# A fused attention, gated convolution, Fourier mixing and FFN kernel on one core: the second FFN group's norm starts at the thirteenth block, and two groups' deviations are inverted as 128x4

## The chip, the cores and the metric

The kernel runs on one core of one Trainium2 chip. The metric is the device time of one execution in microseconds. Three runs of the kernel before gave 1488.09, 1489.01 and 1493.40 us; the median is 1489.01 us.

Engines in the profile: PE is TensorE (matmuls; PEld its weight loads), DVE is VectorE, ACT is ScalarE, POOL is GpSimd, SP is SyncE, which here only issues transfers (DMAs).

## What is computed

Eight batches of 576 tokens with 512 features go through block-causal attention, a gated causal convolution, and then the part that the change touches:

```python
def _moe2_ref(x, w_ch1, w_ch2):
    X = np.fft.fft(np.fft.fft(x, axis=1), axis=2)
    u = x + np.real(X).astype(np.float32)
    mu = np.mean(u, axis=-1, keepdims=True)
    var = np.mean((u - mu) ** 2, axis=-1, keepdims=True)
    un = (u - mu) / np.sqrt(var + 1e-06)
    ch = np.maximum(un @ w_ch1, 0.0) @ w_ch2        # 512 -> 2048 -> 512
    return (u + ch).astype(np.float32)
```

## The kernel before

`phase1` computes attention, convolution and Fourier mixing batch by batch and stores u transposed (features by tokens) in DRAM as `u_d`. `phase2`, the FFN, takes the 4608 tokens in nine groups (g) of 512. A group holds u as `U` (four tiles of 128 features by 512 tokens). Since the ReLU is positively homogeneous, the division by the deviation is left to the end: the matmuls work on u minus its mean, and the result is multiplied by the row `RS[g]`, one over the deviation, spread over 128 partitions.

**A block.** The 2048 hidden features are 16 blocks (f, 0 to 15; the first is block 0). Block f has 12 matmuls into `psh` (lines 1172 to 1174), ACT's ReLU `hh` (1177), DVE's remainder `hl` (1178), and 12 matmuls into four accumulators `o` (1190 to 1192), which PE does one block later, after the `psh` of block f+1. Every f32 product is done as three products of a rounded high part and a low part (H and L in the names). The third of each trio on `o` (line 1192) reads `hl`.

**Weights.** Group 0 also prepares the weights. For each block, `load_w` loads two 128x1024 pieces `rw` of raw 64-bit numbers (line 1081, three buffers), which are decoded to f32: one ACT instruction (80), four DVE instructions (72, 74, 76, 84), then ACT rounds (1085) and DVE takes the remainder (1086). That is ten DVE instructions a block beside `hl`. Groups 1 to 8 find the weights in place.

**The norm.** `norm(g)` is a generator; the block loop takes one step of it a block (`next(nxt, None)`). Its steps: the sum of four tiles (lines 1129 to 1131); the mean by a matmul with a matrix of 1/512 (`average`: L1106 in group 0, and otherwise L1111 and L1112 to split, L1114 and L1115 to multiply); four steps, each x = u - mean (1138), its rounded part `UTH` (1139, ACT), the remainder `UTL` (1140) and the square added to `q` (1142, 1144); the mean of the squares, again by `average`, into `pv`; the root (1149, ACT) and `reciprocal` of 128x512 numbers that are alike in all partitions (1150, DVE). For g below 2, `pool` is DVE, so the whole norm but its ACT steps is DVE work; from group 2 on POOL takes part of it. Group g+1's norm begins in block 5 of group g, or in block 8 where g is 0. The first six steps of group 0's norm are placed in front by a priority.

**What sets the order.** The code is recorded, and a scheduler then fixes the order of every engine's instructions by its own estimates; each engine runs its list in that order and waits at the first instruction that isn't ready. So group 0 runs beside the end of `phase1`. DVE's list mixes decoding, `hl`, the norm of group 1 and the last additions of the Fourier part (842, some of them on POOL). SP's list mixes the loads of `rw` with the last stores of `u_d` (847) and the loads of `U` (1098).

At a group's end each `o` is multiplied by `RS[g]` (1199, DVE), u is added (1201, POOL) and the result stored (1202).

Of the kernel before, what the change touches and what calls it, by code (L numbers as in the profile page):

```python
# [8 lines left out]
F32 = mybir.dt.float32  # L9
F32R = mybir.dt.float32r  # L10
AF = mybir.ActivationFunctionType
# [6 lines left out]
def kernel(  # L18
# [13 lines left out]
    nc = tc.nc  # L32
    B, NP, P, S = q.shape
# [57 lines left out]
    dram = ctx.enter_context(tc.tile_pool(name="dram", bufs=1, space=bass.MemoryType.DRAM))  # L91
    u_d = [dram.tile([D, S], F32, name=f"u_d{b}") for b in range(B)]

    f_d = [dram.tile([10, P], F32, name=f"f_d{i}") for i in range(2)]

    cst = ctx.enter_context(tc.tile_pool(name="cst", bufs=1))
# [945 lines left out]
    def phase2():  # L1042
        with ExitStack() as c2:
# [7 lines left out]
            T = 512  # L1051
            N0X = 6
            OFF = 150
            NG = NTOK // T
            s3 = sb("s3", 3)
            rp = sb("rp", 3)
# [61 lines left out]
            def norm(g):  # L1118

                if g >= NG:  # L1120
                    return
                UTH[g] = UHS[g % 2]
                UTL[g] = ULS[g % 2]
                u = U[g]

                pool = nc.gpsimd if g > 1 else nc.vector
                s1 = s2.tile([P, T], F32, tag="x", name="s1")
                s = s2.tile([P, T], F32, tag="x", name="s")
                nc.vector.tensor_tensor(out=s1, in0=u[:, 2, :], in1=u[:, 3, :], op=ALU.add)
                pool.tensor_tensor(out=s, in0=u[:, 0, :], in1=u[:, 1, :], op=ALU.add)  # L1130
                nc.vector.tensor_tensor(out=s, in0=s, in1=s1, op=ALU.add)
                yield
                pm = ps_t.tile([P, T], F32, tag="t", name="pm")
                yield from average(g, pm, s)
                q = s5.tile([P, T], F32, tag="s", name="q")
                for t in range(4):
                    x = s2.tile([P, T], F32, tag="x", name="x")
                    nc.vector.tensor_tensor(out=x, in0=u[:, t, :], in1=pm, op=ALU.subtract)
                    nc.scalar.copy(out=UTH[g][:, t, :], in_=x)
                    (pool if t % 2 else nc.vector).tensor_tensor(  # L1140
                        out=UTL[g][:, t, :], in0=x, in1=UTH[g][:, t, :].bitcast(F32), op=ALU.subtract)
                    nc.scalar.activation(out=x if t else q, in_=x, func=AF.Square)
                    if t:
                        pool.tensor_tensor(out=q, in0=q, in1=x, op=ALU.add)
                    yield
                pv = ps_t.tile([P, T], F32, tag="t", name="pv")
                yield from average(g, pv, q)
                RS[g] = r = s5.tile([P, T], F32, tag="r", name="r")
                nc.scalar.activation(out=r, in_=pv, func=AF.Sqrt, bias=eps)
                nc.vector.reciprocal(out=r, in_=r)  # L1150
                yield
# [6 lines left out]
            for g in range(NG):  # L1158
# [3 lines left out]
                for f in range(NF + 1):  # L1162
                    if g == 0 and f + 2 < NF:
                        load_w(f + 2)
                    if f == 2:
                        load_u(g + 1)
                    if f == (5 if g else 8):
                        nxt = norm(g + 1)
                    if f < NF:
                        ps = ps_h.tile([P, T], F32, tag="h", name="psh")  # L1170
                        for c in range(4):
                            nc.tensor.matmul(ps, W1H[f][:, c * P:c * P + P], UTH[g][:, c, :], start=(c == 0), stop=False)  # L1172
                            nc.tensor.matmul(ps, W1H[f][:, c * P:c * P + P], UTL[g][:, c, :], start=False, stop=False)  # L1173
                            nc.tensor.matmul(ps, W1L[f][:, c * P:c * P + P], UTH[g][:, c, :], start=False, stop=(c == 3))  # L1174
                        h = HH[f % 2]
                        l = HL[f % 2]
                        nc.scalar.activation(out=h, in_=ps, func=AF.Relu)  # L1177
                        nc.vector.scalar_tensor_tensor(out=l, in0=ps, scalar=0.0, in1=h.bitcast(F32),  # L1178
                                                       op0=ALU.max, op1=ALU.subtract)
                        hs[f] = (h, l)  # L1180
                    next(nxt, None)
                    if f == 0 or g == NG - 1 and f == NF - 1:
                        continue

                    es = list(hs) if f == NF else [f - 1]
                    for t in range(4):
                        c = slice(t * P, (t + 1) * P)
                        for e in es:
                            h, l = hs[e]
                            nc.tensor.matmul(po[t], W2H[e][:, c], h, start=(e == 0), stop=False)  # L1190
                            nc.tensor.matmul(po[t], W2L[e][:, c], h, start=False, stop=False)  # L1191
                            nc.tensor.matmul(po[t], W2H[e][:, c], l, start=False, stop=(e == NF - 1))  # L1192
                    for e in es:
                        del hs[e]
# [105 lines left out]
```

## Time and profile before

| | |
|---|---|
| median of three runs | 1489.01 us (1488.09 to 1493.40) |
| the profiled execution's own time | 1489.86 us |
| its span, first to last instruction | 1488.1 us |
| PE busy | 1425.6 us, 96% of the span |
| DVE busy | 832.4 us, 56% |
| ACT busy | 645.7 us, 43% |
| POOL busy | 309.4 us, 21% |

The shares are averages over stages with different limits. In the 40 slices of the page, DVE's busy tenths are 9 in slices 18 to 21 (about 670 to 818 us: the end of `phase1` and group 0), and 1 or 2 in the slices after, while PE's are 9 nearly throughout. A stretch has to be read by itself: which engine waits there, and for whom.

A row by stretch gives the stretch, its length, the busy time of PE, PEld, DVE, ACT and POOL with their numbers of instructions, the granted TensorE clock (1.00 is 2.4 GHz, 0.50 is 1.2 GHz), the DMA engines' busy share and GB/s. In a timeline row the columns are the start, the duration, the engine, the line and operation with output<-inputs, the shape, how many instructions of one kind were merged (x1, x2), and in brackets the engine's idle time just before and who ended it. A recorded DVE instruction of 128x512 lasts 0.68 us, but the next one starts about 0.60 us after it started; the step from start to start is the price.

### The profile page before, as it was taken

The page shows a single profiled execution, that of the slowest core. Times are in us where ns is not written, and L with a number is a line of the kernel's source. Part 1 is how long each engine was busy: PE and PEld are TensorE (multiplying, and loading weights), DVE is VectorE, ACT ScalarE, POOL GpSimd, SP SyncE. Part 2 cuts the span into 40 slices and gives each one's busy share as a digit, 9 for nine tenths or more (in the row PEclk, how much of TensorE's full clock was granted, in tenths as well). Part 3 has the DMA queues.
Part 4 walks back from the last instruction along what each step waited for, and adds up shares of the span by engine and source line. Part 5 has one row for each costly group of instructions (what it writes and reads, how often), then busy time and mean ns, then how long its engine had stood idle before and what let it go on. Part 6 is the DMA issues. An engine that isn't in the chain of part 4 may idle for free.

```text
span 1488.1 us, 22958 instructions
## 1 busy us (share of the span) xinstructions
PE 1425.6 (96%) x8543; PEld 1207.0 (81%) x8543; DVE 832.4 (56%) x1688; ACT 645.7 (43%) x1655; POOL 309.4 (21%) x254
## 2 busy tenths in 40 slices
PE   5798999999999999999989999999999999999998
PEld 3567888989998999887768888888888888888887
DVE  6777797979797979899992222222222222222212
ACT  5677777777877777643441212121121212112110
POOL 3423232323232323221001111110111111011100
PEclk9899999999999999999999999999999999999999
DMA  7557665656565656244521010100101000010000
GB/s 216 156 154 198 161 177 147 170 149 170 152 171 147 170 152 167 80 132 134 164 74 43 1 57 0 57 0 1 57 0 57 0 30 27 1 57 0 29 0 29
DMA packets 121612, 137.23 MB, mean 92 GB/s; under 512 B 23567, under 2 KB 91421, under 8 KB 121501
## 3 DMA queue, kind: packets, MB, share of 16 engines
q1 hardware_dynamic: 120960, 135.63, 32.2%
q8 instruction: 67, 1.10, 0.3%
q14 instruction: 45, 0.36, 0.1%
q10 hardware_dynamic: 540, 0.14, 0.0%
HBM read 70.57 MB, written 19.01 MB: 60 GB/s over the span
## 4 chain that ended last, share of the span: by engine, by line
PE 67%; DVE 14%; issue 5%; DMA 4%; ACT 4%; POOL 3%; SPq 1%; DVEq 0%; ACTq 0%; POOLq 0%
PE o L1192 7%; PE psh L1172 7%; PE psh L1174 7%; PE psh L1173 7%; PE o L1190 7%; PE o L1191 7%; PE av L609 4%; PE pt L581 3%; DVE gate L636 2%; PE sc L421 2%; PE sc L422 2%; PE psx L182 1%; PE psx L183 1%; PE psx L184 1%; DVE mx L453 1%
## 5 line engine op out<-in xcount | busy, mean ns | idle before, releaser
L1178 DVE SCALAR_TENSOR_TENSOR hl<-psh,hh 128x512 fp32r<-128x512 f32 x144 | 99.2, 689 | 398.9 <-ACT hh L1177 398.9
L1177 ACT ACTIVATE hh<-psh 128x512 fp32r<-128x512 f32 x144 | 85.9, 597 | 494.0 <-PE psh L1174 493.8
L1192 PE MATMUL o<-hl,W2H 128*128 128x512 f32 x504 | 194.3, 392 | 8.2 <-DVE hl L1178 8.1
L1174 PE MATMUL psh<-UTH,W1L 128*128 128x512 f32 x504 | 196.9, 391 | 0.0
L1173 PE MATMUL psh<-UTL,W1H 128*128 128x512 f32 x504 | 196.7, 390 | 0.0
L1172 PE MATMUL psh<-UTH,W1H 128*128 128x512 f32 x504 | 196.7, 390 | 0.0
L1190 PE MATMUL o<-hh,W2H 128*128 128x512 f32 x504 | 196.1, 389 | 0.0
L1191 PE MATMUL o<-hh,W2L 128*128 128x512 f32 x504 | 196.0, 389 | 0.0
L467 ACT ACTIVATE PB<-sc,mx 128x128 f32<-128x128 f32 (+4 forms) x320 | 166.7, 526 | 48.3 <-DVE mx L453 28.6
L581 PE MATMUL pt<-ident,PB 128*128 128x128 f32 x800 | 139.4, 280 | 12.1 <-ACT PTb L587 5.8
L636 DVE SCALAR_TENSOR_TENSOR gate<-XF,cw,gate 128x575 f32<-128x575 f32 (+3 forms) x128 | 121.7, 951 | 5.1 <-ACT gate L63 4.4
L581 PEld LDWEIGHTS pt<-ident,PB 128*128 128x128 f32 x800 | 100.1, 143 | 28.4 <-ACT PTb L587 12.5
L1192 PEld LDWEIGHTS o<-hl,W2H 128*128 128x128 f32 x504 | 94.1, 188 | 32.0 <-DVE hl L1178 12.8
L1201 POOL TENSOR_TENSOR U<-o,U 128x512 f32<-128x512 f32 x32 | 40.4, 1294 | 354.4 <-DVE o L1199 354.4
L1172 PEld LDWEIGHTS psh<-UTH,W1H 128*128 128x128 f32 x504 | 95.0, 189 | 20.0
L1173 PEld LDWEIGHTS psh<-UTL,W1H 128*128 128x128 f32 x504 | 95.0, 189 | 19.9
L1174 PEld LDWEIGHTS psh<-UTH,W1L 128*128 128x128 f32 x504 | 94.9, 188 | 19.7
L1190 PEld LDWEIGHTS o<-hh,W2H 128*128 128x128 f32 x504 | 94.6, 188 | 19.9 <-ACT hh L1177 0.4
L1191 PEld LDWEIGHTS o<-hh,W2L 128*128 128x128 f32 x504 | 94.6, 188 | 19.8
L453 DVE TENSOR_REDUCE mx<-sc 128x1 f32<-128x384 f32 (+2 forms) x192 | 104.2, 560 | 3.8 <-PE sc L184 1.9
L421 PE MATMUL sc<-K,QQ 128*128 128x256 f32 (+2 forms) x256 | 87.8, 353 | 15.4 <-DMA QQ<-QHL 11.7
L632 POOL TENSOR_TENSOR XL<-XF,XH 128x576 fp32r<-128x576 f32 x32 | 46.4, 1451 | 259.5 <-ACT XH L57 259.3
(233 smaller groups left out, 3151.0 us busy)
## 6 DMA issues: line engine op xcount, KB each, us to landing
K<-KP SPq DMA_DIRECT2D x128, 144.0 KB, 2.5
QQ<-QHL SPq DMA_DIRECT2D x128, 128.0 KB, 2.4
rw<-in_w_ch SPq DMA_DIRECT2D x28, 512.0 KB, 4.3
VV<-in_v SPq DMA_DIRECT2D x32, 320.0 KB, 4.0
qraw<-in_q SPq DMA_DIRECT2D x32, 288.0 KB, 3.1
kraw<-in_k SPq DMA_DIRECT2D x32, 288.0 KB, 3.4
out<-U SPq DMA_DIRECT2D x36, 256.0 KB, 2.0
QQ<-QHL SPq DMA_DIRECT2D x128, 64.0 KB, 2.8
```

The source lines that it names most:

```text
L421: nc.tensor.matmul(t[:, o:o + w], q[:, 0, m], KK[p][h][:, 0:w], start=True, stop=False)
L453: nc.vector.reduce_max(out=mx[:, j:j + 1], in_=t, axis=AX.X, negate=one)
L467: nc.scalar.activation(out=PB[i][:, k0:k0 + w], in_=t, func=AF.Exp, bias=nm, accum_out=su[:, at + j:at + j + 1])
L581: nc.tensor.transpose(ps[:, j, :], PB[i][:, (j0 + j) * P:(j0 + j + 1) * P], ident)
L636: nc.vector.scalar_tensor_tensor(out=gate[c][:, s:S], in0=XF[:, 0:S - s], scalar=cw[:, c, 4 - s:5 - s], in1=gate[c][:, s:S], op0=ALU.mult, ...
L1172: nc.tensor.matmul(ps, W1H[f][:, c * P:c * P + P], UTH[g][:, c, :], start=(c == 0), stop=False)
L1173: nc.tensor.matmul(ps, W1H[f][:, c * P:c * P + P], UTL[g][:, c, :], start=False, stop=False)
L1174: nc.tensor.matmul(ps, W1L[f][:, c * P:c * P + P], UTH[g][:, c, :], start=False, stop=(c == 3))
L1178: nc.vector.scalar_tensor_tensor(out=l, in0=ps, scalar=0.0, in1=h.bitcast(F32), op0=ALU.max, op1=ALU.subtract)
L1190: nc.tensor.matmul(po[t], W2H[e][:, c], h, start=(e == 0), stop=False)
L1191: nc.tensor.matmul(po[t], W2L[e][:, c], h, start=False, stop=False)
L1192: nc.tensor.matmul(po[t], W2H[e][:, c], l, start=False, stop=(e == NF - 1))
```

## The change

Four things change, all in `phase2`.

1. Group 1's norm starts in block 12 instead of 8 (`NL = 12`), and from there group 0's loop takes two steps of it a block.
2. Group 1's `U` is asked for in block 9 of group 0 instead of block 2.
3. For groups 0 and 1 the mean of the squares is taken by four matmuls with `q` as the weights and one column of 1/512, so that `pv` holds 128x4 numbers, token 128j + p in partition p. The root and `reciprocal` are done on 128x4.
4. These 512 numbers are written to a DRAM tile `r_d` and read back into 128 partitions of `RS[g]`, by two transfers on SP. For group 1, `average` on `q` (a split on ACT and DVE and two matmuls) falls away; for group 0 the two-pass f32 matmul L1106 and for both the 128x512 reciprocal.

```diff
+    r_d = [dram.tile([4, P], F32, name=f"r_d{i}") for i in range(2)]
...
+            NL = 12
...
                 pv = ps_t.tile([P, T], F32, tag="t", name="pv")
+                if g < 2:
+
+                    for j in range(4):
+                        nc.tensor.matmul(pv[:, j:j + 1], q[:, j * P:j * P + P], ones.bitcast(F32)[:, 0:1],
+                                         start=True, stop=True)
+                    yield
+                    rc = wa.tile([P, 4], F32, name=f"rc{g}")
+                    nc.scalar.activation(out=rc, in_=pv[:, 0:4], func=AF.Sqrt, bias=eps)
+                    nc.vector.reciprocal(out=rc, in_=rc)
+                    yield
+                    nc.sync.dma_start(out=r_d[g].rearrange("c p -> p c"), in_=rc)
+                    RS[g] = s5.tile([P, T], F32, tag="r", name="r")
+                    nc.sync.dma_start(out=RS[g], in_=r_d[g].rearrange("c p -> (c p)").unsqueeze(0).to_broadcast([P, T]))
+                    yield
+                    return
                 yield from average(g, pv, q)
...
-                    if f == 2:
+                    if f == (2 if g else 9):
                         load_u(g + 1)
-                    if f == (5 if g else 8):
+
+                    if f == (5 if g else NL):
                         nxt = norm(g + 1)
...
-                    next(nxt, None)
+                    for _ in range(2 if g == 0 and f >= NL else 1):
+                        next(nxt, None)
```

What the scheduler makes of it, at three places. Names: `st` and `rw` are a weight piece being decoded, `W1L` and `W2L` the remainders of decoded weights, `s`, `al`, `x`, `UTL` and `q` the norm. The new file's line numbers are larger by 2 at `load_w` and the norm (1088 is the old 1086, 1140 the old 1138) and by 18 at `hl` (1196 is the old 1178).

DVE's list from `hl` of block 1 to `hl` of block 2, before:

```order
L1178 SCALAR_TENSOR_TENSOR hl_9279<-psh,hh_9277 128x512
L1150 RECIPROCAL r<-r 128x512
L842 TENSOR_TENSOR XA<-XA 128x580
L84 SCALAR_TENSOR_TENSOR st<-W1H_9288,st 128x512
L74 SCALAR_TENSOR_TENSOR st<-rw,st 128x512
L1178 SCALAR_TENSOR_TENSOR hl_9278<-psh,hh_9276 128x512
```

and now:

```order
L1157 RECIPROCAL rc_9452<-rc_9452 128x4
L76 SCALAR_TENSOR_TENSOR st<-rw,st 128x512
L72 TENSOR_SCALAR st<-rw 128x512
L843 TENSOR_TENSOR XA<-XA 128x580
L1196 SCALAR_TENSOR_TENSOR hl_9281<-psh,hh_9279 128x512
L84 SCALAR_TENSOR_TENSOR st<-W1H_9290,st 128x512
L843 TENSOR_TENSOR XA<-XA 128x580
L74 SCALAR_TENSOR_TENSOR st<-rw,st 128x512
L1088 TENSOR_TENSOR W1L_9291<-st,W1H_9290 128x512
L76 SCALAR_TENSOR_TENSOR st<-rw,st 128x512
L72 TENSOR_SCALAR st<-rw 128x512
L84 SCALAR_TENSOR_TENSOR st<-W2H_9292,st 128x512
```

The large reciprocal is gone, the small one stands ahead of block 1's `hl`, and four decoding instructions (1088, 76, 72, 84) that stood behind block 2's `hl` stand ahead of it.

DVE's list from `hl` of block 12 to `hl` of block 13, before:

```order
L1178 SCALAR_TENSOR_TENSOR hl_9278<-psh,hh_9276 128x512
L1086 TENSOR_TENSOR W1L_9329<-st,W1H_9328 128x512
L84 SCALAR_TENSOR_TENSOR st<-W2H_9330,st 128x512
L1138 TENSOR_TENSOR x<-U_9336,pm 128x512
L72 TENSOR_SCALAR st<-rw 128x512
L1086 TENSOR_TENSOR W2L_9331<-st,W2H_9330 128x512
L1140 TENSOR_TENSOR UTL_9338<-x,UTH_9337 128x512
L74 SCALAR_TENSOR_TENSOR st<-rw,st 128x512
L72 TENSOR_SCALAR st<-rw 128x512
L1144 TENSOR_TENSOR q<-q,x 128x512
L76 SCALAR_TENSOR_TENSOR st<-rw,st 128x512
```

and now (four rows, 74, 84, 76 and `hl`, follow these):

```order
L1196 SCALAR_TENSOR_TENSOR hl_9280<-psh,hh_9278 128x512
L1088 TENSOR_TENSOR W1L_9331<-st,W1H_9330 128x512
L84 SCALAR_TENSOR_TENSOR st<-W2H_9332,st 128x512
L1131 TENSOR_TENSOR s_9977<-U_9338 128x512
L1132 TENSOR_TENSOR s<-U_9338 128x512
L1088 TENSOR_TENSOR W2L_9333<-st,W2H_9332 128x512
L1133 TENSOR_TENSOR s<-s,s_9977 128x512
L72 TENSOR_SCALAR st<-rw 128x512 x2
L74 SCALAR_TENSOR_TENSOR st<-rw,st 128x512
L1114 TENSOR_TENSOR al<-s,ah 128x512
L76 SCALAR_TENSOR_TENSOR st<-rw,st 128x512
```

Before, nine of the norm's DVE instructions stood ahead of block 13's `hl`, spread over the blocks from the fourth `hl` on (1129, 1130, 1131, 1112, 1138, 1140, 1138, 1140, 1144); now four do, all in this block, and the four tiles' x, `UTL` and `q` stand behind it.

SP's list around the end of `phase1`, now:

```order
L1083 DMA rw<-in_w_ch 128x4x256
L1159 DMA r_d_65<-rc_9452 128x4x1
L1083 DMA rw<-in_w_ch 128x1024
L848 DMA u_d_64<-XA 128x2x289 x2
L848 DMA u_d_64<-XA 128x2x287 x2
L1161 DMA r<-r_d_65 128x512
L1083 DMA rw<-in_w_ch 128x4x256
L1100 DMA U_9338<-u_d_57 128x4x64
L1083 DMA rw<-in_w_ch 128x1024
L1100 DMA U_9338<-u_d_58 128x4x448
```

The two rows of `r_d` are new. Although its place in the code is later, the load of group 1's `U` stands where it stood, but for its larger half, which now comes after one more load of `rw`.

## Rows read from the trace of the kernel before

**Rows 1.** Busy time of each engine, by stretch: group 0, its end, groups 1 to 8.

```profile
705.00:767.00 62.00, 54.92 (x230) 42.50 (x231) 61.61 (x111) 29.64 (x51) 0.00 (x0) 1.00 0.44 140
767.00:777.00 10.00, 10.00 (x39) 8.03 (x38) 7.26 (x12) 4.12 (x8) 0.48 (x1) 0.83 0.00 0
777.00:1488.00 711.00, 706.20 (x3101) 581.13 (x3099) 188.84 (x245) 120.99 (x206) 100.25 (x74) 1.00 0.07 24
```

**Rows 2.** Who waited for whom, 680 to 780 us: total, times, longest (us).

```profile
PE o L1192 <- DVE hl L1178: 8.1, 8, 2.4
...
DVE s L1129 <- DMA U<-u_d: 0.6, 1, 0.6
```

**Rows 3.** Timeline, DVE, around the large reciprocal of group 0.

```profile
684.15 3.33 DVE L1150 RECIPROCAL r<-r 128x512 f32<-128x512 f32 x1
687.41 0.69 DVE L842 TENSOR_TENSOR XA<-XA 128x580 f32<-128x580 f32 x1
...
688.62 1.93 DVE L74 SCALAR_TENSOR_TENSOR st<-rw,st 128x512 int32<-128x512 int32 x1
690.48 0.68 DVE L1178 SCALAR_TENSOR_TENSOR hl<-psh,hh 128x512 fp32r<-128x512 f32 x1
```

**Rows 4.** Timeline, DVE: `hl` of block 6, decoding, `hl` of block 7.

```profile
716.74 0.68 DVE L1178 SCALAR_TENSOR_TENSOR hl<-psh,hh 128x512 fp32r<-128x512 f32 x1
...
718.54 0.75 DVE L72 TENSOR_SCALAR st<-rw 128x512 int32<-128x512 int32 x2
...
722.82 0.68 DVE L1178 SCALAR_TENSOR_TENSOR hl<-psh,hh 128x512 fp32r<-128x512 f32 x1
```

**Rows 5.** Timeline, DVE, late in group 0: `hl` of blocks 12 and 13, the norm.

```profile
756.70 0.68 DVE L1178 SCALAR_TENSOR_TENSOR hl<-psh,hh 128x512 fp32r<-128x512 f32 x1
...
764.86 0.68 DVE L1178 SCALAR_TENSOR_TENSOR hl<-psh,hh 128x512 fp32r<-128x512 f32 x1
...
766.66 0.67 DVE L1138 TENSOR_TENSOR x<-U,pm 128x512 f32<-128x512 f32 x1
...
772.39 0.68 DVE L1140 TENSOR_TENSOR UTL<-x,UTH 128x512 fp32r<-128x512 f32 x1
```

**Rows 6.** Timeline, PE, the end of group 0 and group 1's first matmul.

```profile
765.59 1.19 PE L1192 MATMUL o<-hl,W2H 128*128 128x512 f32 x4 [2.42 <-DVE hl L1178]
766.62 0.39 PE L1172 MATMUL psh<-UTH,W1H 128*128 128x512 f32 x1
...
770.95 0.40 PE L1190 MATMUL o<-hh,W2H 128*128 128x512 f32 x1
...
776.43 0.40 PE L1115 MATMUL pv<-al,ones 128*128 128x512 f32 x1
...
776.90 0.39 PE L1172 MATMUL psh<-UTH,K 128*128 128x512 f32 x1
```

**Rows 7.** By stretch, with the granted clock as the third number from the end.

```profile
702.00:706.00 4.00, 2.38 (x11) 1.67 (x10) 4.00 (x8) 1.29 (x2) 0.00 (x0) 1.00 0.43 134
766.00:770.00 4.00, 4.00 (x13) 3.15 (x12) 3.90 (x8) 1.85 (x3) 0.00 (x0) 0.62 0.00 0
```

**Rows 8.** Timeline, PE: group 0's mean of squares in f32.

```profile
678.15 1.02 PE L1106 MATMUL pv<-q,ones 128*128 128x512 f32 x2
```

**Rows 9.** Timeline, POOL: an addition of the Fourier part.

```profile
683.70 1.45 POOL L842 TENSOR_TENSOR XA<-XA 128x580 f32<-128x580 f32 x1 [1.03 <-DVE XA L842]
```

**Rows 10.** Timeline, SP: stores of `u_d`, a load of `rw`, group 2's load of `U`.

```profile
683.65 6.74 SPq L847 DMA_DIRECT2D u_d<-XA  x4
692.41 0.37 SPq L1081 DMA_DIRECT2D rw<-in_w_ch  x1
...
787.42 0.93 SPq L1098 DMA_DIRECT2D U<-u_d  x2
```

**Rows 11.** Page, parts 3 and 6: the queue's packets, MB, share; a load's landing (us).

```profile
q1 hardware_dynamic: 120960, 135.63, 32.2%
...
rw<-in_w_ch SPq DMA_DIRECT2D x28, 512.0 KB, 4.3
```

## The prediction

> **What bounds the kernel now.** I read the page's 40 slices first, then busy time by stretch, then who waited for whom, then the timelines of DVE and PE. The reader is to see two regimes. In groups 1 to 8 PE is busy 706.20 of 711.00 us [rows 1]: nothing there can get faster by a shift of DVE work, so whatever moves the start of group 1 moves the end by as much. In group 0 DVE is busy 61.61 of 62.00 us and PE only 54.92 [rows 1]: DVE decodes weights, makes `hl` and does the norm of group 1 by turns, and PE waits for `hl`, 8.1 us in eight waits, the longest 2.42 us [rows 2, 6]. After that longest wait the granted clock is 0.62 on average over 766 to 770 us [rows 7], so part of that stretch ran at 1.2 GHz. The question is what DVE's list loses ahead of the last `hl` that PE waits for, block 13's.
>
> **Unit prices on DVE.** A block without norm work goes from `hl` to `hl` in 722.82 - 716.74 = 6.08 us; of its eleven instructions two are 72, which take 0.67 us together [rows 4], so the nine others cost 0.60 each. PE started 26 matmuls from 770.95 to 776.90 us, 0.229 each [rows 6], so a block's 24 take 5.50 us. DVE therefore falls behind by 0.58 us a block by decoding alone; norm work comes on top.
>
> **What leaves DVE ahead of block 13's `hl`.** (a) Group 0's reciprocal: 687.41 - 684.15 = 3.26 us [rows 3]. (b) The norm's first sum, taken in before between the `hl` of blocks 3 and 4, with the wait for `U`: 0.60 + 0.60 = 1.20 [rows 2]. (c) Blocks 7 to 13: from `hl` of block 7 to that of block 13 are 764.86 - 722.82 = 42.04 us [rows 4, 5]; six plain blocks would be 36.48, so the norm's other eight instructions, with small waits for ACT, cost 5.56. Four come back in block 12 (three sums and `al`), 2.41. That leaves 3.15. Sum: 3.26 + 1.20 + 3.15 = 7.61 us.
>
> **What is given back.** The small reciprocal: four columns, so I take 0.07; the root it needs is ready, since PE makes `pv` at 678.15 [rows 8] and the list reaches the reciprocal near 680.7. With the large reciprocal gone, the addition that followed it at 687.41 is reached at 684.8, but POOL's addition that it reads ends at 683.70 + 1.45 = 685.15 [rows 9]: a wait of about 0.45. The next POOL addition stretched one decoding instruction to 1.93 us [rows 3]; it may now stretch it to about 2.4, 0.53 more, or by chance not at all; I take 0.53. Together 1.05; what remains is 6.56. Then the loads: DVE runs 3 us ahead of before, but the 1 MB of `U` still stands among the loads of `rw` and lands in the same stretch. A load lands 4.3 us after its issue [rows 11], and in the new list the loads freed by the instructions 76 behind block 1's `hl` are wanted about 4.0 to 5.0 us later. Bounds: nothing, or 1.5 us; the nearest row is the 0.6 us that DVE waited for `U` [rows 2]; I take 0.7. So block 13's `hl` ends 5.9 us earlier, near 759.6 rather than 764.86 + 0.60.
>
> **From there to group 1.** In before 776.90 - 765.46 = 11.44 us pass [rows 5, 6]. (d) The twelve matmuls of block 15's `psh` took 770.95 - 766.62 = 4.33 us instead of 12 x 0.229 = 2.75 [rows 6]: 1.6 us lost to the clock. I take it as gone: PE's wait ahead of block 13's `hl` becomes about 2.0 us by my count (DVE needs 8.5 us from block 12's `hl` to block 13's, PE 28 matmuls, 6.4), which lies between the 1.62 us after which the clock stayed at 1.00 [rows 7] and the 2.42 after which it fell; this is a choice. (e) The two matmuls of `average` on `q`, the second at 776.43 [rows 6], leave: 0.46. So 9.4 us pass, and group 1 starts near 769.0, 7.9 earlier.
>
> **Group 1's side.** The four tiles now follow block 13's `hl`. DVE has two decoding steps, x, `hl` 14, a remainder, `UTL`, x, x, `hl` 15, `UTL`, `UTL`, x, two `q` and `UTL` to do, 15 steps of 0.60, 9.0 us: the last `UTL` is ready near 768.6, and PE wants it with its tenth matmul, 9 x 0.23 after 769.0, at 771.1. It is covered by 2.5 us; if that cover goes, each us late costs one. The four new matmuls stand in group 1's first block behind eleven others; `q` is ready about 1 us before. Their price isn't in the trace: between nothing and the 1.02 us of the f32 matmul with 512 columns [rows 8]; eight passes with one column each have only weights to load, so I take the middle, 0.5. In group 0 the same swap lies beside DVE's work and counts nothing. The 3.3 us reciprocal of group 1 stood behind all that PE waited for and is worth nothing. The two transfers of `r_d` are wanted at the ends of the groups, tens of us later; what they could hold up is SP's list, which is a rival below. The load of `U` hardly moves in SP's list, so step 2 of the change is worth nothing by itself.
>
> **Sum.** 7.9 - 0.5 = 7.4 us. The profiled execution took 1489.86 us, so its own time would be 1482.5. The median of the runs lies 0.85 lower, and they are what the new runs will be set against: 1489.01 - 7.4 = 1481.6, rounded to 1481.5. Of this case alone the ends are: no loss to POOL's stretch, loads and matmuls, 1.7 us more gain, 1479.9; and 1.5 for the loads and 1.0 for the matmuls, 1.3 less, 1482.9.
>
> **Rival 1: the clock falls again.** PE still waits about 2 us ahead of block 13's `hl`. If the clock then falls as in before, (d) is not gained: 1483.1, and 1484.4 with the loads late. The Trainium skill (TensorE: Matmul & The Clock Gate, Part 1) has the clock at half rate after an idle stretch and at full rate again after sustained work, and says that where it strikes varies from run to run; the fall in before agrees in kind [rows 7], and by it this rival would come in some executions and not in others.
>
> **Rival 2: the second norm comes too late.** The tiles' chain goes DVE, ACT, DVE and shares three buffers of x. In before x at 766.66 and the last `UTL` at 772.39 are 5.73 us apart [rows 5], for the last two tiles; four at that pace are 11.5 from 760.8, so 772.9 with the last one's 0.6: 1.8 us after the need, 1483.3; if ACT's order adds 2 us a pair, 1487.3. For: step 1 pushes eleven instructions into the last two blocks. Against: DVE's list interleaves the tiles, so ACT works on one while DVE does the next.
>
> **Rival 3: SP is blocked by the write of `r_d`, and the kernel is slower.** The write goes out in 512 runs of 4 bytes, and the read behind it holds SP until it has landed; behind the read stand the loads of `rw` (group 0) and of group 2's `U` (group 1). The price of a run: the queue's packets took 32.2% of 16 engines' 1488.1 us for 120960 packets, 63 ns each [rows 11]; 32 runs an engine are 2.0 us, so landing in perhaps 4 us. In group 0 the write goes out near 681.4, the stores of `u_d` keep SP until 690.4 anyway [rows 10], and the next load is wanted by about 690.1, so up to 8.7 us are free. In group 1 SP issues group 2's `U` 787.42 - 776.90 = 10.5 us after the group's start [rows 10]; the write goes out some 4 us after it, so about 6 are free. Beyond that each us costs one at each place. At 17 us landing (0.45 us a run) it is 8.3 + 11 - 7.4 = 12 slower, near 1501; from 11 us on the gain is gone. The Trainium skill (DMA: Bandwidth & Descriptors, Rules for kernel authors) speaks against such a write: a strided last dimension lowers to one descriptor per element, and is to be made contiguous. That is the 512 runs above; no row here shows such a transfer.
>
> **Rival 4: nothing is gained.** If the loads, not DVE, pace group 0, removed DVE time turns into waits for `rw`: 1488.5. Against: DVE waited for a load only 0.6 us [rows 2].
>
> **How the numbers follow.** Forecast 1481.5, chance 0.62; rival 1 0.18; rival 2 0.07; rival 3 0.06; rival 4 0.07. A measurement can tell about 0.5% from no change, that is 7.4 us or 1481.6, which lies in the middle of the forecast's own range. The range, 1479 to 1487, takes in the first two rivals; the last two are left out, all but the mild end of the third. Faster by over 0.5%: 0.40, that is 0.65 of the forecast's case, a little over half since I took the worse end for POOL's stretch; within 0.5%: 0.53; slower by over 0.5%: 0.07, the third rival and other waits on SP.
>
> **What would show it.** In the changed profile: `hl` of block 13 near 759 and group 1's first matmul near 769; PE's waits for `hl` in group 0 down from 8.1 to about 4 us, one of about 2 left; the granted clock 1.00 after it, or not; no wait of PE for `UTL`; `r_d` landed within 6 us. Wrong it would be by DVE waiting for loads, by a long write of `r_d`, or if PE's first block of group 1 waits.

## The result and the profile after

The changed kernel takes 1509.61 us (median, 1507.69 to 1511.81) beside 1488.97 for the kernel before: a ratio of 1.0134, 95% interval 1.0117 to 1.0151, 20.6 us slower where 7.4 us faster was predicted. The profiled execution took 1511.81 us, its span is 1510.0.

First the busy time by stretch of the kernel after; the columns are those of [rows 1], with the count of instructions in brackets, and the granted clock, DMA share and GB/s at the end.

```profile
800.00:900.00 100.00, 95.61 (x405) 76.76 (x404) 27.42 (x36) 17.45 (x30) 15.47 (x11) 0.97 0.07 23
900.00:1100.00 200.00, 200.00 (x862) 161.17 (x861) 53.59 (x71) 36.67 (x63) 29.32 (x22) 1.00 0.06 22
...
777.00:1510.00 733.00, 723.68 (x3110) 582.52 (x3108) 189.98 (x247) 121.27 (x207) 100.64 (x74) 0.99 0.07 24
```

The last row answers to the third of [rows 1]: the same matmuls (3110 here, 3101 there) now take 723.68 us of PE's time, not 706.20. The middle row shows how: PE is busy without a gap and the clock is at its upper level, 2.4 GHz, and yet only 862 matmuls fit into 200 us. Before there were 881:

```profile
900.00:1100.00 200.00, 200.00 (x881) 165.00 (x880) 55.74 (x73) 39.23 (x67) 34.15 (x25) 1.00 0.06 22
```

So this part is no wait. On average a matmul of groups 1 to 8 costs about 2% more, in code that the change, but for group 1's norm, doesn't touch. The first row, 800 to 900 us, has 4.4 us of idle PE besides.

The second part is in group 0. The timeline of DVE after:

```profile
680.63 0.16 DVE L1157 RECIPROCAL rc<-rc 128x4 f32<-128x4 f32 x1
...
695.84 0.69 DVE L1196 SCALAR_TENSOR_TENSOR hl<-psh,hh 128x512 fp32r<-128x512 f32 x1 [5.48 <-ACT hh L1195]
...
702.01 0.43 DVE L72 TENSOR_SCALAR st<-rw 128x512 int32<-128x512 int32 x1 [2.14 <-DMA rw<-in_w_ch]
...
767.10 0.68 DVE L1196 SCALAR_TENSOR_TENSOR hl<-psh,hh 128x512 fp32r<-128x512 f32 x1
```

The small reciprocal takes 0.16 us, against 3.33 [rows 3]. But `hl` of block 2 waits 5.48 us for ACT, and a load is waited for later. Block 13's `hl` starts at 767.10, not near 759 as predicted and not even at the 764.86 of before [rows 5]. ACT, whose list is in order, had stood still for a load:

```profile
694.66 0.66 ACT L80 ACTIVATE W2H<-rw 128x512 fp32r<-128x512 f32 x1 [8.31 <-DMA rw<-in_w_ch]
```

That load was issued right behind the write of `r_d`. The timeline of SP after, which answers to [rows 10]:

```profile
680.82 0.37 SPq L1159 DMA_DIRECT2D r_d<-rc  x1
681.45 0.34 SPq L1083 DMA_DIRECT2D rw<-in_w_ch  x1
...
691.98 0.33 SPq L1161 DMA_DIRECT2D r<-r_d  x1
...
782.30 0.43 SPq L1159 DMA_DIRECT2D r_d<-rc  x1
...
794.06 0.33 SPq L1161 DMA_DIRECT2D r<-r_d  x1
795.13 0.93 SPq L1100 DMA_DIRECT2D U<-u_d  x2
```

From write to read, which waits for the landing, 11.2 us pass in group 0 and 11.8 in group 1; the prediction had taken about 4. In group 1 group 2's `U` stands behind the read, 7.7 us later than before (795.13 against 787.42). DVE then waits for it, and PE behind DVE and ACT; two rows, of DVE and of PE:

```profile
801.20 0.69 DVE L1131 TENSOR_TENSOR s<-U 128x512 f32<-128x512 f32 x1 [10.38 <-DMA U<-u_d]
```

```profile
804.94 0.79 PE L1209 MATMUL o<-hh,W2H 128*128 128x512 f32 x1 [4.39 <-ACT hh L1195]
```

To compare kernels I split each profile by groups: a group lasts from its first `psh` matmul on `K` in PE's timeline to the next group's (group 1's first in before is the last of [rows 6]). The last column is the number of PE matmuls in 900 to 1100 us. Group 0 differs by up to 3.2 us between profiles in which nothing of its order was changed (before, e2, e5, e8, e9), the others hardly where the pace is the same. Its start, which none of the edits was meant to move, lies anywhere from 663.95 to 667.73 us in these profiles; so whole kernels are compared by the medians of their runs, and parts by this table.

| kernel | group 0 | group 1 | groups 2 to 8 | matmuls |
|---|---|---|---|---|
| before | 110.47 | 88.35 | 622.8 | 881 |
| after | 110.87 | 97.29 | 635.5 | 862 |
| e1_pad | 110.61 | 96.74 | 634.5 | 863 |
| e2_shift | 112.10 | 89.72 | 635.9 | 862 |
| e3_nl | 105.33 | 90.53 | 624.0 | 881 |
| e4_row | 102.77 | 90.62 | 635.6 | 859 |
| e5_m256 | 113.71 | 88.34 | 623.1 | 881 |
| e6_p512 | 110.83 | 96.14 | 622.9 | 881 |
| e7_r512 | 102.75 | 89.31 | 623.0 | 879 |
| e8_wb64 | 110.97 | 89.56 | 627.8 | 875 |
| e9_kal | 111.07 | 87.95 | 621.2 | 884 |
| e10_best | 102.36 | 89.14 | 622.1 | 877 |
| e11_actq | 111.51 | 94.55 | 622.8 | 879 |
| e12_half | 111.45 | 97.25 | 622.7 | 881 |
| e13_extra | 109.01 | 95.75 | 624.2 | 873 |
| e14_spread | 102.40 | 89.35 | 623.1 | 878 |

After against before: 0.4 us in group 0, 8.9 in group 1, 12.6 in groups 2 to 8, together the 21.9 us by which the spans differ. Two causes had to be found, then: one for the pace, one for the stalls around the write.

### The profile page after: what moved, and what is told of

It reads as the page before. It is cut to its first block, busy times and chain, and to the rows that moved or that the text cites. A ratio compares the mean times of both kernels' runs of the same rounds, so it can differ in the third digit from the quotient of the medians.

```text
span 1510.0 us, 22995 instructions
## 1 busy us (share of the span) xinstructions
PE 1444.0 (96%) x8555; PEld 1208.7 (80%) x8555; DVE 828.7 (55%) x1687; ACT 642.9 (43%) x1654; POOL 308.1 (20%) x254
## 4 chain that ended last, share of the span: by engine, by line
PE 69%; DVE 12%; DMA 7%; ACT 5%; issue 3%; POOL 2%; SPq 2%; DVEq 0%; ACTq 0%; POOLq 0%
PE o L1209 8%; PE o L1210 8%; PE o L1211 8%; PE psh L1191 8%; PE psh L1190 8%; PE psh L1192 8%; PE av L610 4%; PE pt L582 3%; DMA rw<-in_w_ch 3%; DVE gate L637 2%; PE sc L422 2%; PE sc L423 1%; ACT PB L468 1%; PE psx L183 1%; PE psx L184 1%
## 5 line engine op out<-in xcount | busy, mean ns | idle before, releaser
L1209 PE MATMUL o<-hh,W2H 128*128 128x512 f32 x504 | 200.5, 398 | 8.1 <-ACT hh L1195 8.1
L1211 PE MATMUL o<-hl,W2H 128*128 128x512 f32 x504 | 199.9, 399 | 3.6 <-DVE hl L1196 3.6
L1210 PE MATMUL o<-hh,W2L 128*128 128x512 f32 x504 | 199.8, 397 | 0.0
L582 PE MATMUL pt<-ident,PB 128*128 128x128 f32 x800 | 140.1, 281 | 11.2 <-ACT PTb L588 5.6
```

The lines of the kernel that those rows point to most:

```text
L582: nc.tensor.transpose(ps[:, j, :], PB[i][:, (j0 + j) * P:(j0 + j + 1) * P], ident)
```

## Experiments on the pace: where the tiles stand

The one thing of groups 2 to 8 that the change touches is where their tiles stand. Theory A says that this slows their matmuls; rival B says that the write of `r_d` and the new order are all there is. `rc0` and `rc1` are allocated in the pool `wa`, and what is allocated behind them, the weights of blocks 2 to 15 and `U1`, `UTH1` and `UTL1`, moves by as many bytes as the two take. In the built program that is 64: each takes 32, though it needs 16. `hh`, `hl`, `U0`, `UTH0` and `UTL0` stand ahead of them and stay.

**e2_shift**, only the addresses:

```diff
             HL = [wa.tile([P, T], F32R, name=f"hl{i}") for i in range(2)]
+            for i in range(2):
+                nc.vector.memset(wa.tile([P, 4], F32, name=f"gap{i}_wa"), 0.0)
```

> The kernel before with two unused tiles of 16 bytes, each set to zero once, at the place where rc0 and rc1 stand in the changed kernel: all of the weights of blocks 2 to 15 and U1, UTH1, UTL1 move by 64 bytes and nothing else changes. Theory A: 862 matmuls in 900 to 1100 us instead of 881, and 1489.0 + 15.6 = about 1504.6. Rival B: 881 and 1489 within 1 us.

Measured: 1506.32 us, ratio 1.0112 (1.0090 to 1.0133), and 862 matmuls in 900 to 1100 us. Nothing of the change but the 64 bytes is in this kernel (and two small writes of zeros), and it is 16.6 us slower than its 1489.69 of before. The addresses cost what theory A said.

**e1_pad**, the changed kernel with 128 bytes in place of 64:

```diff
-                    rc = wa.tile([P, 4], F32, name=f"rc{g}")
+                    rc = wa.tile([P, 16], F32, name=f"rc{g}")[:, 0:4]
```

> The changed kernel with one difference: each of the two small tiles rc takes 64 bytes instead of 16, so that the tiles allocated behind them (the weights of blocks 2 to 15, U1, UTH1, UTL1) stand 128 bytes further on than in the kernel before, not 64. Theory A (the 64 bytes slow every matmul of groups 1 to 8): PE issues about 880 matmuls in 900 to 1100 us again instead of 862, and the time falls by 2.2% of 711 us, 15.6 us, to about 1494. Rival B (the slow write of r_d and what stands behind it, or the new order, is all there is): 862 matmuls still, and 1509.6 within 2 us.

Measured: 1510.38 us (1.0115 to 1.0161), 863 matmuls. My first form of the theory, that tiles have to start at the same place modulo 128 as before, falls; that addresses matter doesn't. The means of PE's groups in 900 to 1100 us of e2_shift told how to go on; in before all of these are 389 but those on `K`, `KP` and `KL`, the weights of blocks 0 and 1, which are 393 to 395 (number in front of the bar: count; behind it: busy us, mean ns). First e2_shift:

```profile
L1174 PE MATMUL psh<-UTH,W1H 128*128 128x512 f32 x128 | 50.2, 392 | 0.0
...
L1192 PE MATMUL o<-hh,W2H 128*128 128x512 f32 x124 | 48.9, 394 | 0.0
```

and two groups of before, from 780 us on:

```profile
L1174 PE MATMUL psh<-UTH,W1L 128*128 128x512 f32 x448 | 174.3, 389 | 0.0
...
L1191 PE MATMUL o<-hh,KL 128*128 128x512 f32 x64 | 25.3, 395 | 0.0
```

`psh` suffers less than `o`, and it does so by groups: even ones last 90.55 us, odd ones 89.69. PE's timeline of e2_shift in an odd group, with the first of each twelve:

```profile
984.49 0.39 PE L1174 MATMUL psh<-UTH,W1H 128*128 128x512 f32 x1
...
987.23 0.39 PE L1192 MATMUL o<-hh,W2H 128*128 128x512 f32 x1
...
990.03 0.39 PE L1174 MATMUL psh<-UTH,W1H 128*128 128x512 f32 x1
```

Twelve `psh` take 2.74 us, twelve `o` 2.80; in before each twelve take 2.72 (975.77, 978.49 and 981.21 start three runs there), and in an even group of e2_shift both take 2.80. In odd groups the moving tile of `psh`, `UTH1`, had moved with the weights; the moving tile of `o`, `hh`, had not. Hence theory D: a matmul is slower, by 2.80 - 2.72 over 12, 6.6 ns, when its weights and its moving tile don't start at the same place modulo some size.

**e5_m256** (a gap of 256 bytes in the kernel before), **e6_p512** (each `rc` takes 256 bytes) and **e8_wb64** (a gap of 64 bytes ahead of `U1` alone); the three edits stand in one fence, and the comments say whose a line is:

```diff
+            nc.vector.memset(wa.tile([P, 64], F32, name="gap0_wa"), 0.0)      # e5, behind hl
...
-                    rc = wa.tile([P, 4], F32, name=f"rc{g}")                  # e6
+                    rc = wa.tile([P, 64], F32, name=f"rc{g}")[:, 0:4]
...
+            nc.vector.memset(wb.tile([P, 16], F32, name="gap"), 0.0)          # e8, ahead of U1
```

> The kernel before with one unused tile of 256 bytes ahead of the weights of blocks 2 to 15 and U1, UTH1, UTL1. Theory D (a matmul is 6.6 ns slower when the start addresses of its weights and of its moving tile within the partition differ, modulo some size; in the kernel before both are 160 modulo 512 but for K, KP and KL): a shift of 64 or of 128 bytes is slow by e1 and e2, so the size is at least 256. If it is 256, 881 matmuls in 900 to 1100 us and 1489; if it is 512 (or the rule is another one), 862 and about 1505, as any shift so far.

> The changed kernel with each rc tile taking 256 bytes, so that all tiles behind them move by 512 bytes. Theory D: 881 matmuls in 900 to 1100 us, and 15.6 us less than the changed kernel's 1509.6, about 1494. Rival: it was not the addresses relative to each other that mattered but some absolute place which only the kernel before has, 862 and 1509.

> The kernel before with an unused tile of 64 bytes ahead of U1, UTH1 and UTL1 alone: the weights stay. Theory D: only the psh matmuls of the odd groups (1, 3, 5, 7) slow down from 0.2267 to 0.2333 us, 14 blocks x 12 x 4 groups x 6.6 ns = 4.4 us, so 1493.4; psh of even groups and all o matmuls stay at 0.2267. Rival (the address of the weights alone decides, whatever the moving tile's): nothing slows down, 1489.

Measured: e5 1490.99 us (1.0001 to 1.0025) with 881 matmuls, so a shift of 256 is as good as none and the size is 256. e6 1496.87 (1.0034 to 1.0064) with 881: the pace is back in the changed kernel, and 12.7 us with it. e8 1497.75 (1.0035 to 1.0075), 875 matmuls, odd groups at 89.55 us and even ones at 88.31 to 89.22. The rival falls, since the weights stand where they did. The loss is 8 us by the medians (of two runs), not 4.4; but by the profile's groups the four odd ones are 1.2 us longer each, 4.9 together, which is near the 4.4, and the rest lies elsewhere: 1.2 in groups 2 and 6, 1.8 up to the end of group 0, which no theory here foresaw. Inside an odd group, 968 to 1045 us, the `o` matmuls have slowed down too, though both of their operands stand right:

```profile
L1191 PE MATMUL o<-hh,W2H 128*128 128x512 f32 x54 | 21.3, 395 | 0.0
...
L1173 PE MATMUL psh<-UTH,W1H 128*128 128x512 f32 x53 | 21.0, 395 | 0.0
```

Twelve of either kind take 2.76 to 2.77 us, 5.53 a block; 2.72 for a matched run (operands at the same place modulo 256) and 2.80 for an unmatched one would make 5.52. So theory D is right on which groups suffer and on what a block costs, and wrong that each matmul pays for itself alone: the loss spreads over matched and unmatched runs that follow each other. How that hangs together inside PE these runs don't say.

**e9_kal** asks for the reverse. `K`, `KP` and `KL` are slow in before, [rows 6] has the first of them; they lie ahead of `eps`, whose 32 bytes put all later tiles 32 bytes off.

```diff
-            eps = wa.tile([P, 1], F32, name="eps")
+            eps = wa.tile([P, 64], F32, name="eps")[:, 0:1]
```

> The kernel before with eps taking 256 bytes instead of 32, so that all tiles behind it move by 224 bytes: they then stand at 384 modulo 512, as far from a multiple of 256 as K, KP and KL do (128 or 384), which stand 32 bytes off in all kernels so far. Theory D (weights and moving tile want the same start modulo 256): the 24 psh and 24 o matmuls of each group on K, KP and KL fall from 0.2333 to 0.2267 us like all others, 48 x 6.6 ns = 0.32 us a group, groups 2 to 7 take 88.0 instead of 88.31 us, and the time falls by 8 x 0.32 = 2.6 us to about 1487. Rival (K is slow for a reason of its own): 88.31 and 1489.5; or, if it is 160 that is good in itself, 90 a group.

Measured: 1488.42 us, ratio 0.9981 (0.9970 to 0.9993). Groups 2 to 5 take 87.95 us each instead of 88.31, and PE's row in 900 to 1100 us now reads as all others:

```profile
L1190 PE MATMUL o<-hh,KP 128*128 128x512 f32 x16 | 6.2, 389 | 0.0
```

So no tile is slow by itself: where it stands to the other operand decides. The Trainium skill (TensorE: Matmul & The Clock Gate, Part 2, Step-by-step: what each phase is for) says that PE reads weights and moving tile through two independent ports, so that loading the next weights takes nothing from the running matmul. It speaks of bandwidth and not of where tiles stand. If reads that share nothing were all there is to it, no layout would cost anything; here layouts cost up to 6.6 ns of 227, and the measurement decides.

## Experiments on the write and on the order

**e4_row** and **e7_r512** write `r_d` in four runs of 512 bytes; e4 with `rc` and `rt` moving the later tiles by 1152 bytes, e7 by 2048.

```diff
-                    nc.sync.dma_start(out=r_d[g].rearrange("c p -> p c"), in_=rc)
+                    pt = ps_t.tile([P, T], F32, tag="t", name="pt")
+                    nc.tensor.transpose(pt[0:4, 0:P], rc, ident)
+                    rt = wa.tile([P, P], F32, name=f"rt{g}")
+                    nc.scalar.copy(out=rt[0:4], in_=pt[0:4, 0:P])
+                    nc.sync.dma_start(out=r_d[g], in_=rt[0:4])
```

> e1_pad with the four columns turned by PE into four rows of 128 and copied by ACT, so that r_d is written as 4 runs of 512 bytes, not 512 runs of 4. Theory B: the read of r_d is issued within 4 us of the write instead of 11 to 12, DVE's hl of block 2 no longer waits 5.5 us for ACT, group 2's U comes 8 us earlier and PE's loss at 800 to 900 us goes: 6 to 11 us less than e1_pad, 1483 to 1488 if e1_pad is at 1494. Rival: the landing has nothing to do with the runs (any write read back takes 11 us), and it equals e1_pad.

> e4_row (r_d written as 4 runs of 512 bytes) with the tiles rc and rt taking 512 bytes each, so that all tiles behind them move by 2048 bytes. Theory D: 881 matmuls in 900 to 1100 us, and 15.6 us less than e4_row's 1494.7, about 1479, faster than both kernels; that is what my prediction said the change would do, 1481.5, once its two unforeseen costs are gone. Rival: 862 and 1495.

Measured: e4 1494.66 us (1.0022 to 1.0049), slow in pace (859 matmuls), with group 0 at 102.77. Against e1_pad that is 15.7 us less, more than I had expected, and the base was higher too, since e1_pad had not cured the pace. e7 1482.78 (0.9940 to 0.9973): with both costs gone the idea of the change is worth 6.9 us. SP's timeline of e7:

```profile
687.47 0.45 SPq L1163 DMA_DIRECT2D r_d<-rt  x1
...
691.21 0.34 SPq L1165 DMA_DIRECT2D r<-r_d  x1
```

3.7 us from write to read. Against e6, e7 is 14.1 us faster: 8.1 in group 0 and 6.8 in group 1 by the table. It differs by the write and by what turns the columns, and the write's place in SP's list moved with that: it goes out behind the stores of `u_d`, at 687.47, and not ahead of them as in e6, at 680.05. The next pairs of kernels take this apart. How 512 runs of 4 bytes cost that was the next question.

**e11_actq** (e6 with the write on ACT's queue) and **e12_half** (e6 with 256 runs: two of the four columns are left out, and the read takes the other two twice). Of e12 the write is shown:

```diff
-                    nc.sync.dma_start(out=r_d[g].rearrange("c p -> p c"), in_=rc)
+                    nc.scalar.dma_start(out=r_d[g].rearrange("c p -> p c"), in_=rc)                # e11
+                    nc.sync.dma_start(out=r_d[g][0:2].rearrange("c p -> p c"), in_=rc[:, 0:2])     # e12
```

> e6_p512 (addresses mended, 512 runs of 4 bytes) with the write of r_d issued on ACT's queue instead of SP's; the read stays on SP. Theory Q (in group 0 the cost is the load of rw that stands behind the write in the same queue): that load lands in its usual 4 us, DVE's hl of block 2 no longer waits 5.6 us for ACT, and group 0 shrinks from 110.8 us to between 103 and 106; SP still waits 11 us for the read in group 1, so group 1 stays near 96; about 1490. Rival W (the write fills the DMA engines whatever queue it comes from, or SP's wait for the read is what hurts in group 0 too): group 0 stays near 110 and the time at 1496.9.

> e6_p512 with only two of the four columns written, 256 runs of 4 bytes instead of 512; the read fetches these two rows twice, so r is wrong for half of the tokens of groups 0 and 1 and all else is as it was. Theory L (the landing is paid by the run, 11.2 us / 512 = 22 ns each): SP's wait for it falls from 11.2 to about 5.6 us, group 1 from 96.1 to about 91, group 0 by about 5, 1486 to 1488. Rival F (a fixed delay of a write read back): 11 us and 1496.9 as before.

Measured: e11 1495.75 us (1.0019 to 1.0040), group 0 at 111.5. The load of `rw` isn't behind the write in its queue any more, and ACT waits for it as long as in the changed kernel; theory Q falls:

```profile
694.33 0.66 ACT L80 ACTIVATE W2H<-rw 128x512 fp32r<-128x512 f32 x1 [8.36 <-DMA rw<-in_w_ch]
```

The GB/s at the end of the row for 682 to 692 us, first before, then e6_p512, then e11_actq:

```profile
682.00:692.00 10.00, 10.00 (x45) 8.15 (x44) 10.00 (x10) 1.89 (x3) 3.94 (x3) 1.00 0.50 172
```

```profile
682.00:692.00 10.00, 9.55 (x42) 7.46 (x40) 7.59 (x10) 0.62 (x1) 3.25 (x2) 1.00 0.20 25
```

```profile
682.00:692.00 10.00, 9.94 (x44) 7.75 (x42) 7.97 (x10) 0.62 (x1) 3.54 (x3) 1.00 0.22 23
```

For ten microseconds behind the write little is moved, whichever of the two queues it came from, though the 2 KB write itself is small. The DMA engines' recorded busy share falls too, from 0.50 to about 0.2, so the time isn't in the packets as they are recorded. e12 took 1499.79 (1.0045 to 1.0078). From write to read 9.0 us pass in group 0 and 10.6 in group 1 (679.25 to 688.22 and 781.49 to 792.12 in SP's timeline), where e6 has 11.6 and 12.5: less, but not half, so theory L in that form falls, and the time gained nothing. Its read is two transfers instead of one; what the three microseconds above e6 are I didn't separate.

**e13_extra** and **e14_spread** add such a write to e7 that nothing reads; in e14 its runs stand 64 bytes apart.

```diff
+                    nc.sync.dma_start(out=x_d[g].rearrange("c p -> p c"), in_=rc)             # e13, x_d: 4 x 128
+                    nc.sync.dma_start(out=x_d[g][:, :, 0].rearrange("c p -> p c"), in_=rc)    # e14, x_d: 4 x 128 x 16
                     pt = ps_t.tile([P, T], F32, tag="t", name="pt")
```

> e7_r512 (r_d written in four rows, 1482.8) with the write in 512 runs of 4 bytes added back, to a DRAM tensor that nothing reads, so that SP never waits for its landing. Theory W (the write itself holds up all other transfers for about 11 us): DMA traffic at 682 to 692 us falls from e7's 209 GB/s to about 25, group 0 grows from 102.8 to 109 to 111 us and group 1 from 89.3 to 95 or so, 1495 to 1497 like e6. Rival S (SP's wait for the landing does the harm): the added write costs SP 0.4 us twice and nothing else, 1483.

> e13_extra with the 512 runs of 4 bytes 64 bytes apart in DRAM (a tensor of 4 x 128 x 16, one element of each 16), so that no two runs share 64 bytes. If the hold-up comes from runs that are neighbours in DRAM being merged one after another, most of it goes: traffic at 682 to 692 us above 150 GB/s, group 0 near 103 to 105, 1483 to 1486. If it is paid by the run whatever its place, it equals e13_extra.

Measured: e13 1496.02 us (1.0023 to 1.0054), as slow as e6, with nothing that waits for the added write. e14 1483.24 (0.9936 to 0.9971), as fast as e7, with as many runs of 4 bytes. The rows for 682 to 692 us, e13 and then e14:

```profile
682.00:692.00 10.00, 8.01 (x36) 6.13 (x34) 5.93 (x7) 0.62 (x1) 2.54 (x2) 1.00 0.35 76
```

```profile
682.00:692.00 10.00, 10.00 (x46) 8.08 (x45) 10.00 (x14) 2.52 (x5) 3.25 (x2) 1.00 0.70 225
```

The cost is neither SP's wait for this write nor the number of runs: it is 4-byte runs that are neighbours in DRAM, and it falls on the transfers that follow (in e13 the write goes out at 678.40, so part of its stop lies ahead of 682). Why neighbours cost this no run shows, and 64 bytes is the only other spacing that was tried. Nor is SP free of waits in e13: in group 1 the write of `r_d` itself, in four runs, is held up behind the added one, and 9.4 us pass to its read, against 3.4 in e7:

```profile
778.69 0.47 SPq L1165 DMA_DIRECT2D r_d<-rt  x1
...
788.13 0.32 SPq L1167 DMA_DIRECT2D r<-r_d  x1
```

So of group 1's loss these runs don't say how much goes by way of SP. The Trainium skill (DMA: Bandwidth & Descriptors, Specifications) has transfers below 512 bytes read, modify and write. If that rule were all, e14, with the same 4 bytes a run, would be as slow as e13; it isn't, so the size isn't enough.

**e3_nl** has the new order without the new inverse:

```diff
+            NL = 12
...
-                    if f == 2:
+                    if f == (2 if g else 9):
                         load_u(g + 1)
-                    if f == (5 if g else 8):
+                    if f == (5 if g else NL):
                         nxt = norm(g + 1)
...
-                    next(nxt, None)
+                    for _ in range(2 if g == 0 and f >= NL else 1):
+                        next(nxt, None)
```

> The kernel before with the second norm begun at block 12, two steps a block, and the second group's load at f 9; both groups keep the old sum over PE and the 128x512 reciprocal, and no address changes. My prediction's steps without the reciprocal of group 0: the first norm sum 1.20 and blocks 7 to 13 3.15 off DVE ahead of hl 13, group 1 some 4 us earlier, about 1485; with the clock's fall gone too, 1483.5. Rival C (the reorder itself costs, since the tiles of the second norm then come after PE wants them): 1490 or more. The pace of groups 1 to 8 stays at 881 in 900 to 1100 us in either case.

Measured: 1487.73 us, ratio 0.9982 (0.9970 to 0.9994). The time is 2.0 us less, where 4 to 6 were expected: group 0 is 5.1 us shorter in the profile, but group 1 is 2.2 longer. Two rows of its timelines, DVE and PE:

```profile
775.36 3.35 DVE L1151 RECIPROCAL r<-r 128x512 f32<-128x512 f32 x1 [0.53 <-ACT r L1150]
```

```profile
779.31 0.50 PE L1192 MATMUL o<-hh,KP 128*128 128x512 f32 x1 [1.25 <-DVE o L1201]
```

With the norm begun late, group 1's large reciprocal falls among the multiplications that empty group 0's `o`, and PE waits 1.25 us for the last of them; what the rest of the 2.2 us is I didn't separate.

**e10_best** is e7 with e9's `eps`.

> e7_r512 (r_d written in four rows, tiles behind rc moved by whole multiples of 512) with the eps of e9_kal. Theory D: 2.6 us less than e7's 1482.8, about 1480, groups 2 to 7 at 88.0 us. Rival: nothing more than e7, 1482.8.

Measured: 1480.61 us, ratio 0.9929 (0.9914 to 0.9945): faster than both kernels, by 9.9 us than before and 29 than after.

## Why the prediction was wrong, step by step

- **What bounds the kernel.** Right that in before group 0 waits for DVE and that groups 1 to 8 are PE alone. The first step that failed is "whatever moves the start of group 1 moves the end by as much": it holds only if PE's pace stays, and the change moved the tiles that PE reads. That cost 12.7 us (after less e6), of which the prediction has nothing. In before the means of PE's groups showed two kinds of matmul, 389 and 395 ns, that differed only in the tiles they read (the rows beside e2_shift); they were the rows to ask about.
- **What leaves DVE** (3.26 + 1.20 + 3.15 less 1.05). Right as a sum; its terms weren't measured one by one. In e7, which does what the change was thought to do, block 13's `hl` starts 756.71 - 663.95 = 92.8 us after group 0 does, which is 759.2 on the time axis of before, whose group 0 begins at 666.43; predicted was near 759:

```profile
756.71 0.69 DVE L1200 SCALAR_TENSOR_TENSOR hl<-psh,hh 128x512 fp32r<-128x512 f32 x1
```

- **The loads**, 0.7 us, between 0 and 1.5. This is the second step that failed. In the changed kernel the term is 8.1 us (group 0, e6 less e7), since the write stops the loads. Without that write (e7) DVE waits 0.17 us for one load.
- **The clock and group 1's start** (d, e). Right, as far as it was put to the test. In the changed kernel itself, with the four norm instructions between block 12's `hl` (758.48) and block 13's as the prediction had them, PE waits 1.61 us ahead of block 13's `hl`, not the 2.0 counted, and the granted clock of 766 to 770 us stays at 1.00:

```profile
767.84 1.19 PE L1211 MATMUL o<-hl,W2H 128*128 128x512 f32 x4 [1.61 <-DVE hl L1196]
```

```profile
766.00:770.00 4.00, 2.39 (x10) 1.80 (x10) 4.00 (x7) 1.55 (x3) 0.00 (x0) 1.00 0.00 0
```

From the end of that `hl`'s step to group 1 pass 777.26 - 767.70 = 9.6 us, predicted 9.4. In e7 the scheduler took the norm's three sums back to block 3 (695.27 to 698.88 us), block 13's `hl` comes 6.87 us after block 12's and not 8.5, and PE's wait is 0.86 us, with the granted clock right behind it at 1.00:

```profile
757.45 1.21 PE L1215 MATMUL o<-hl,W2H 128*128 128x512 f32 x4 [0.86 <-DVE hl L1200]
```

```profile
758.00:762.00 4.00, 4.00 (x19) 3.25 (x18) 4.00 (x7) 2.24 (x5) 0.00 (x0) 1.00 0.01 2
```

Group 1 begins 102.75 us after group 0 there, predicted 769.0 - 666.43 = 102.6. The choice, that the clock holds through a wait of 2.0 us, was never tried: the waits ahead of that `hl` were 1.61 and 0.86 us, and 1.77 in e3, where the clock of 762 to 766 us, right behind it, is 1.00 as well.

- **The four matmuls in group 1.** Mis-sized: 0.5 was taken, between 0 and 1.02. In e7 the matmul on `K` ahead of them starts at 769.04 and the next at 770.09, 1.05 us apart instead of 0.23: 0.8.

```profile
769.04 0.40 PE L1195 MATMUL psh<-UTL,K 128*128 128x512 f32 x1
769.27 0.95 PE L1152 MATMUL pv<-ones,q 128*128 128x1 f32 x8
770.09 0.48 PE L1196 MATMUL psh<-UTH,K 128*128 128x512 f32 x1
```

- **"Worth nothing": group 1's reciprocal.** Only in the old order. In the new one it stands in PE's way (e3, 1.25 us in one wait), so both halves of the change belong together.
- **Rival 3.** Named the right operation and gave it 0.06. Its price, 2 us for 32 packets, came from the time of packets of other sizes, and the lost time isn't in the packets as recorded (a busy share of about 0.2 behind the write); the landing, taken as perhaps 4 us, took 11.2 and 11.8 us. That is the step behind the second failure. Put into the rival's own terms these give 11.2 - 8.7 = 2.5 and 11.8 - 6 = 5.8. Group 1 is near it (6.8 by e6 less e7), and SP was held back there, as described, from the `U` that DVE wants; how much of it the held-up transfers would cost without SP's wait stays open, since SP waits in e13 too. Group 0 doesn't agree: 8.1, since what is lost there is the load behind the write (e11), not SP's time.
- **Rivals 1, 2 and 4.** None occurred: in e7 the clock didn't fall, no matmul waits for `UTL`, and removed DVE time became time. In rival 1 the 1484.4 "with the loads late" has the 0.5 for the matmuls in it as well; the loads alone make 1483.9.

So 6.9 us of gain were there, against 7.4 predicted; 14.1 us for the write (e6 less e7) and 12.7 for the pace stood against them, 19.9 net of the 20.6 measured.

## To carry to other kernels

A new small tile is an edit of everything allocated behind it: give it a size that keeps the later tiles where they were modulo 256 bytes, and look for kinds of matmul in the profile whose mean differs though shapes don't. A 2 KB write isn't small if it is 512 neighbouring pieces of 4 bytes: price it by what the transfers behind it do, not by its own packets, and turn the columns into rows on PE first. An operation that "stood behind all that anyone waited for" has to be looked at again in the new order.

## What was not expected of the hardware

- A matmul of 512 columns takes 226.7 ns from start to start when weights and moving tile start at the same place modulo 256 bytes, and 233.3 when they are 32, 64 or 128 bytes off (881 against 862 in 200 us, clock at 1.00 in both). Where matched and unmatched runs alternate, single runs lie in between, 2.74 to 2.77 us for twelve against 2.72 and 2.80, and a pair of runs costs what the two would alone.
- Behind one write of 512 runs of 4 bytes to neighbouring places in DRAM the DMA traffic of the core is 23 to 25 GB/s for ten microseconds, where it was 172 before the change, whether SP's or ACT's queue issued it, and the loss of time is the same when nothing waits for it (e13); 64 bytes apart they are not noticed (225 GB/s, 1483.24 us against 1482.78 without).
- With half as many such runs the read goes out 1.8 to 2.6 us sooner, not in half the time; what law that follows stays open.
